# Top-k attention and a mixture of experts on one core: where the second fold and the row scatters stand in the early slots

## The chip, the core and the metric

The kernel runs on one core of a Trainium2 chip. The core has a matrix engine (PE), a vector engine (DVE), an activation engine (ACT), a general engine (POOL, also called GpSimd) and a queue for transfers (SP). Each works through its own list of instructions in a fixed order, and they meet through semaphores. What counts is the time of one execution on the device, in microseconds (us). It was 1285.07 us as the median of three runs, from 1283.54 to 1285.09.

## The reference

Two stages are computed one after the other, in float32.

- Attention over 8 batches, 8 heads, 576 positions and 64 values per head. For each row of scores the 32 largest of 576 are kept, all others are masked, and the softmax of the kept ones weighs the rows of `v`.
- A mixture of 8 experts on the 4608 resulting rows of 512 values. A gate picks one expert for each row; that expert is two matrix products (512 to 1024, relu, 1024 to 512), and the result is scaled by the gate's probability.

```python
scores = scale * np.matmul(q, k.transpose(0, 1, 3, 2))
kth = np.partition(scores, -top_k, axis=-1)[..., -top_k:-top_k + 1]
scores = np.where(scores >= kth, scores, -1000000000.0)
...
for e in range(E):
    h = np.maximum(x_sorted[lo:hi] @ w1[e], 0.0)
    y_sorted[lo:hi] = h @ w2[e]
```

## The kernel before

Two heads make a unit, so a batch has four units. The score rows of two units are cut into nine groups of two tiles of 128 rows by 576 scores; with 8 batches there are 144 groups. The loop at the end of the kernel (`loop`) takes one group per pass. A pass is called a slot here, and slots are counted from 0; slot i searches the thresholds of group i.

**The search on DVE.** The 576 scores of a row are not searched directly. `fold` (L314) takes the larger and the smaller of two halves (L320 `h`, L321 `l`, 288 wide). `fold_on` (L323) folds `h` once more: L327 puts the larger of its two halves (144 wide) into `few`, and the smaller into `hl`. The smaller half is either a minimum on DVE (L335), or, where `aside_too` is set, one sum and one difference on POOL (L332, L333), on the bits as whole numbers. `lists` (L356) then adds the eight largest of `l` and of the two halves of `hl` to `few`. `search` (L358) finds 32 maxima in four rounds: MAX8 for both tiles (L379), then MATCH_REPLACE8 for both tiles (L390), which takes the found ones out. The last MAX8 gives the threshold.

While group i is searched, the folds of group i+1 are placed in between. `behind` runs L320 and L321 ahead of the search. `then` is the second fold, `fold_on`. It stands in round 1, straight behind that round's two MAX8, if `soon` is set, and ahead of the last round otherwise.

**What follows the threshold.** ACT turns it into `low` (L401) and computes `w` (L417). POOL subtracts twice (L426, 128 by 576 each) and notes the doubtful rows (L407); at the start of the next slot it writes `nbias` (L385). ACT takes the exponent (L434), PE transposes and multiplies.

**What is fixed in order.** PE, ACT and DVE run in the order in which the loop writes their instructions. POOL's instructions are chained in that order too (`in_turn`), and its transfers are tied behind the last POOL instruction.

**The early slots.** `QUIET` is 66: in slots 1 to 65 `loose` is set. A slot is `heavy` when a unit's rows are due in it: POOL then scales the unit's logits and output rows (L519 to L524, L533) beside the search. That is so, from slot 8 on, in the slots whose number modulo 9 is 3 or 8. `k.crowded` is set by each scatter, store and block of rows. `soon` is set in an early slot that is heavy or does not follow a crowded one, and POOL takes the fold's last step where `soon` is set and the slot is not heavy, which is the case in 37 slots.

**Scatters and stores.** When a batch's four units are done, five scatters (L601, indirect transfers that POOL issues) put its rows into `x_rows`, sorted by expert. `scatter(1)` issues one at the end of each slot from slot 24, 42, 60 and so on. A finished expert block leaves its output store (L888, also POOL's) in `stores`; `put_stores` issues what is there, at the end of each slot. Pieces of the expert products fill PE beside the attention, and what is left of them runs when the attention is over.

Of the kernel before, what the change touches and what calls it, by code (L numbers as in the profile page):

```python
# [44 lines left out]
def kernel(  # L45
# [54 lines left out]
    NC = 4  # L100
# [7 lines left out]
    NT = 2 * NC + 1  # L108
# [25 lines left out]
    k = SimpleNamespace()  # L134
# [217 lines left out]
    def lists(f):  # L352

        for m in range(2):
            for j, away in enumerate((f.l[:, m, :], f.hl[:, m, 0:QF // 2], f.hl[:, m, QF // 2:QF])):
                nc.vector.max(out=f.few[:, m, QF + 8 * j:QF + 8 * j + 8], in_=away)  # L356

    def search(tiles, s, f, then=lambda: None, soon=False, behind=lambda: None, beside=lambda: None):  # L358

        m_all = range(2)  # L360
        tops = k.small.tile([P, 2, TOP_K], F32, name="tops", bufs=4)
        if k.exact:
            src = [s[:, m, :, :].rearrange("p j k -> p (j k)") for m in m_all]
            width = S
        else:
            src = [f.few[:, m, 0:QF] for m in m_all]
            width = LW
            if not f.aside:
                lists(f)
        behind()  # L370
        scr = k.att.tile([P, 2, width], F32, name="scr", bufs=1)
        nbias = k.small.tile([P, 2], F32, name="nbias", bufs=3)
        R = TOP_K // 8

        for r in range(R):
            if r == R - 1 and not soon:
                then()
            for m in m_all:
                nc.vector.max(out=tops[:, m, r * 8:(r + 1) * 8], in_=src[m])  # L379
                if r > 1:  # L380
                    tick()
            if r == 1 and soon:
                then()
            if r == 0:
                in_turn(nc.gpsimd.tensor_scalar_mul(nbias, tops[:, :, 0], -scale))  # L385
                beside()
            if r < R - 1:
                for m in m_all:
                    first = r == 0 and not k.exact
                    nc.vector.match_replace(  # L390
                        out=src[m] if first else scr[:, m, :], in_to_replace=tops[:, m, r * 8:(r + 1) * 8],
                        in_values=src[m], imm_value=NEG,
                    )
                    if r > 1:
                        tick()
                    src[m] = f.few[:, m, :] if first else scr[:, m, :]
                if first and f.aside:
                    lists(f)
        thr = tops[:, :, TOP_K - 1]
        low = k.small.tile([P, 2], F32, name="low", bufs=3)  # L400
        nc.scalar.activation(low, thr, AF.Copy, scale=STEEP)  # L401

        def doubts():
            n, i = tiles[0]
            at = n.b * U + n.u
            over = doubt[:, at:at + 2, 2 * NC, :] if tails(tiles) else doubt[:, at, 2 * i:2 * i + 2, :]
            k.last_pool = in_turn(nc.gpsimd.tensor_tensor(  # L407
                over, f.few[:, :, QF + 7:LW:8], _inner(thr, NL), op=ALU.subtract
            )).ins

        return low, nbias, doubts
# [607 lines left out]
    QUIET = 66  # L1019
# [4 lines left out]
    with fast:  # L1024
# [10 lines left out]
        waiting, loaded, coming, spare, scatters, stores = [], [], [], [], [], []  # L1035
        current = None
        left = clock = 0

        def level(b):

# [22 lines left out]
                loaded[-1].at = clock  # L1063

        def put_stores():
            while stores:
                k.crowded = True
                stores.pop(0)()

# [139 lines left out]
        def at_place(name):  # L1209
            for end in list(late):  # L1210
                if end[1] == name:
                    end[1] = next(end[0], None)
                    if end[1] is None:
                        late.remove(end)
# [18 lines left out]
        def loop():  # L1233
            nonlocal credit, rate, clock
            for i in range(min(AHEAD, len(work))):
                multiply(i)
                s_of[i], steps = scores(got_of.pop(i))
                for step in steps:
                    step()
            multiply(AHEAD)  # L1240
            for step in prepared:
                step()
            for odd in range(2):
                for h in range(2):
                    r = slice(h * D, (h + 1) * D)
                    at = odd * (lw + P) + h * E
                    nc.vector.tensor_copy(turn[r, :, at:at + E], wg[r, odd::2, :])
            f_of[0] = fold(s_of[0], (slice(0, 1), slice(1, 2)))
            fold_on(f_of[0])
            for i, (b, g) in enumerate(work):  # L1250
                tiles = tiles_of(i)
                u, tile = g[0]
                if tile == 0 and u % 2 == 0:
                    open_unit(tiles[0][0])
                if tails(tiles):
                    open_unit(tiles[1][0])

                loose = 0 < i < QUIET
                k.heavy = loose and "rows" in [place for _, place in late]
                soon = loose and (k.heavy or not k.crowded)  # L1260
                then = behind = beside = lambda: None
                if i + 1 < len(work):
                    def behind():
                        f_of[i + 1] = fold(s_of[i + 1])

                    then = lambda: fold_on(f_of[i + 1], soon and not k.heavy)
                    if i:
                        behind()
                        behind = lambda: None
                if k.heavy:  # L1270
                    beside = lambda: at_place("rows")
                held = k.heavy and k.crowded
                low, nbias, doubts = search(tiles, s_of[i], f_of.pop(i), then, soon, behind, beside)
                k.crowded, k.heavy = held, False
                at_place("small")
                w_of[i] = depths(s_of[i], low)
                less(s_of.pop(i), w_of[i])
                doubts()
                at_place("pool")
                if not loose:  # L1280
                    at_place("relu")
                    at_place("rows")
                put_stores()
                scatter(1)
                at = i % per_batch
                if at == FIRST and b:
                    rate = level(b) * PIECES / (U * NT)
                credit += rate * len(g)
                room = left
                if b == B - 1 and at >= ARRIVED:  # L1290
                    room -= KEEP
                    credit = room / (len(work) - i)
                share = {0: 0.5, 1: 1.2, 2: 1.6, 3: 0.5, 2 * NC: 1.4}[tile]
                now = max(0, min(int(credit * share + 0.5), room))
                credit -= now
                clock = i
                if i + AHEAD < len(work):
                    s_of[i + AHEAD], steps = scores(got_of.pop(i + AHEAD))
                    for step in steps:
                        step()  # L1300
                if loose:
                    at_place("relu")
                evacuate()
                at_place("turn")
                turns = turning(i - 1) if i else iter(())
                next(turns, None)
                part = min(BETWEEN, now - now // 2)
                rest = pieces(part)
                next(turns, None)
                rest = pieces(now - now // 2 - part + rest)  # L1310
                weights(tiles, w_of[i], nbias)
                next(turns, None)
                evacuate()
                if i + AHEAD + 1 < len(work):
                    multiply(i + AHEAD + 1)
                if tile == NC - 1:
                    end = ending(b, u)
                    late.append([end, next(end)])
                at_place("products")
                at_place("weights")  # L1320
                credit = min(credit + pieces(now // 2 + rest), 6 * rate)

            k.between = True
            for _ in turning(len(work) - 1):
                pieces(1)
            assert len(late) == 1
            clock = None
            for place in late[0][0]:
                if place == "rows":
                    pieces(4)  # L1330
            kept = left - (SURE + HALVES + PLAIN) * PIECES
            assert kept >= 0, kept
            k.apart = True
            pieces(kept)
# [139 lines left out]
```

## Time and profile before

| what | value |
|---|---|
| median of three runs | 1285.07 us |
| the profiled execution's own time | 1284.61 us |
| its span, first to last instruction | 1283.0 us |
| PE busy | 1176.1 us (92%) |
| DVE busy | 1058.8 us (83%) |
| ACT busy | 933.3 us (73%) |
| POOL busy | 732.0 us (57%) |
| L327, second fold, 144 times | 0.557 us on average, 0.426 to 1.535 |
| L332, POOL's first fold step, 37 times | 0.792 us on average |
| L426, POOL's subtraction, 288 times | 1.441 us on average |
| L407, doubtful rows, 144 times | 0.379 us on average |
| L601, scatter, 40 times | 1.065 us on average |
| L888, store, 37 times | 1.052 us on average |

The span is what the profile covers; the execution's own time has 1.6 us more around it. An engine is busy while one of its instructions has started and not ended, so a stalled instruction counts as busy. Instructions of one engine overlap a little at their ends. A timeline line gives the start, the time, the engine, the line of the code, what is written from what, and how many were merged; an idle time ahead of the instruction stands in brackets with what ended it.

### The profile page before, as it was taken

How to read it: one execution, taken by the hardware profiler on the slowest of the kernel's cores; microseconds unless marked ns; L12 is line 12 of the kernel's file. 1: busy time of each engine (PE TensorE's matmuls, PEld its weight loads, DVE VectorE, ACT ScalarE, POOL GpSimd, SP SyncE). 2: the span in 40 equal slices, each digit the busy share in tenths (PEclk: the TensorE clock that was granted, in tenths of full speed). 3: DMA queues.
4: the chain of work that ended last, by engine and by line, in shares of the span. 5: the costliest groups of instructions: out<-in, count | busy, mean ns of one | idle time of the engine just before them, and what ended most of it. 6: DMA issues, size and time to landing. Idle time of an engine off the chain costs nothing. (4 is left out here: it accounts for less than half of the span.)

```text
span 1283.0 us, 24461 instructions
## 1 busy us (share of the span) xinstructions
PE 1176.1 (92%) x7574; PEld 823.6 (64%) x7574; DVE 1058.8 (83%) x4608; ACT 933.3 (73%) x2136; POOL 732.0 (57%) x884
## 2 busy tenths in 40 slices
PE   6767767898899999999999999999999999999998
PEld 3444444665566566667666666666666667789975
DVE  8999999999999999999999999999999965000000
ACT  4888887988799888888788888888888872112121
POOL 4777777786678665658555855676557743101010
PEclk9888788999899999999999999999999999999999
DMA  5001113741474147533946464547555548996582
GB/s 153 31 30 31 31 39 126 263 157 39 146 251 162 39 150 283 182 135 98 332 142 218 163 224 153 189 146 264 178 178 202 172 149 285 353 358 235 215 301 83
DMA packets 98701, 220.81 MB, mean 172 GB/s; under 512 B 5309, under 2 KB 26301, under 8 KB 98560
## 3 DMA queue, kind: packets, MB, share of 16 engines
q1 hardware_dynamic: 91360, 198.87, 44.5%
q0 software_dynamic: 6384, 19.97, 4.2%
q8 instruction: 61, 1.00, 0.3%
q14 instruction: 80, 0.66, 0.2%
q10 hardware_dynamic: 816, 0.31, 0.1%
HBM read 195.75 MB, written 24.04 MB: 171 GB/s over the span
## 5 line engine op out<-in xcount | busy, mean ns | idle before, releaser
L426 POOL TENSOR_TENSOR w<-s,w 128x576 f32<-128x576 f32 x288 | 409.2, 1441 | 317.5 <-ACT w L417 317.4
L979 PE MATMUL ph<-xTs,w 128*128 128x128 f32 x2112 | 263.0, 278 | 2.6 <-ACT xTs L870 2.6
L979 PEld LDWEIGHTS ph<-xTs,w 128*128 128x128 f32 x2112 | 251.3, 194 | 21.1 <-issue 17.6
L996 PE MATMUL py<-w,hT 128*128 128x512 f32 x528 | 248.7, 600 | 1.9 <-ACT hT L984 1.6
L434 ACT ACTIVATE w<-w,nbias 128x576 f32<-128x576 f32 x288 | 223.0, 785 | 2.3 <-POOL w L426 1.4
L445 PE MATMUL wTm<-turn,w 128*128 128x128 f32 x1152 | 173.9, 291 | 52.7 <-ACT oT L484 29.1
L417 ACT ACTIVATE w<-s,low 128x576 f32<-128x576 f32 x288 | 207.7, 768 | 4.7
L304 PE MATMUL sc<-qkb 64*128 64x288 f32 (+1 forms) x1280 | 200.7, 465 | 7.8 <-DMA qkb<-in_qk_dram 4.0
L445 PEld LDWEIGHTS wTm<-turn,w 128*128 128x128 f32 x1152 | 135.1, 148 | 111.6 <-ACT oT L484 35.5
L311 ACT COPY s<-sc 128x576 f32<-128x576 f32 x288 | 168.0, 634 | 11.9 <-PE sc L304 11.8
L379 DVE MAX8 tops<-scr 128x8 f32<-128x168 f32 x576 | 169.5, 328 | 0.0
L452 ACT COPY wT<-wTm 128x512 f32<-128x512 f32 x256 | 140.7, 596 | 37.8 <-PE wTm L445 37.2
L379 DVE MAX8 tops<-few 128x8 f32<-128x144 f32 (+1 forms) x576 | 154.9, 314 | 0.0
L304 PEld LDWEIGHTS sc<-qkb 64*128 64x128 f32 (+1 forms) x1280 | 107.1, 190 | 71.5 <-issue 35.2
L996 PEld LDWEIGHTS py<-w,hT 128*128 128x128 f32 x528 | 92.0, 191 | 86.5 <-issue 83.0
L482 PE MATMUL po<-wT,vb 128*64 128x288 f32 x1024 | 143.8, 425 | 0.0
L888 POOL DMA_INDIRECT out_dram<-y,xg x37 | 38.9, 1052 | 161.3 <-ACT y L1005 82.0
L356 DVE MAX8 few<-l 128x8 f32<-128x288 f32 x288 | 129.8, 451 | 0.0
L320 DVE TENSOR_TENSOR h<-s 128x576 f32<-128x576 f32 (+1 forms) x145 | 111.7, 770 | 3.9 <-ACT s L311 3.6
L321 DVE TENSOR_TENSOR l<-s 128x576 f32<-128x576 f32 (+1 forms) x145 | 114.3, 788 | 0.0
L482 PEld LDWEIGHTS po<-wT,vb 128*64 128x64 f32 x1024 | 70.1, 141 | 68.9 <-issue 17.4
L356 DVE MAX8 few<-hl 128x8 f32<-128x72 f32 x576 | 102.3, 221 | 0.0
(205 smaller groups left out, 1596.7 us busy)
## 6 DMA issues: line engine op xcount, KB each, us to landing
w<-in_moe_w_dram SPq DMA_DIRECT2D x74, 2048.0 KB, 9.2
qkb<-in_qk_dram SPq DMA_DIRECT2D x31, 608.0 KB, 3.8
vb<-in_v_dram SPq DMA_DIRECT2D x32, 320.0 KB, 3.2
xg<-x_rows SPq DMA_DIRECT2D x37, 257.0 KB, 9.1
x_rows<-blank SPq DMA_DIRECT2D x13, 257.0 KB, 7.9
x_rows<-blank POOLq DMA_DIRECT2D x4, 257.0 KB, 9.8
x_rows<-x,posi POOLq DMA_INDIRECT x40, 3.2
out_dram<-y,xg POOLq DMA_INDIRECT x37, 3.9
```

Of the source, the lines that this page charges most:

```text
L304: nc.tensor.matmul(ps[rows, j, 0:HF], n.q[d, cols], n.k[d, keys], start=True, stop=True)
L311: lambda m=m, ps=ps: nc.scalar.copy(s[:, m, :, :], ps[:, :, 0:HF]) for m, ps in enumerate(got)
L356: nc.vector.max(out=f.few[:, m, QF + 8 * j:QF + 8 * j + 8], in_=away)
L379: nc.vector.max(out=tops[:, m, r * 8:(r + 1) * 8], in_=src[m])
L417: nc.scalar.activation(w[:, m, :], s[:, m, :, :].rearrange("p j k -> p (j k)"), AF.Relu, scale=-STEEP, bias=low[:, m:m + 1],)
L426: k.last_pool = in_turn(nc.gpsimd.tensor_tensor(w[:, m, :], s[:, m, :, :].rearrange("p j k -> p (j k)"), w[:, m, :], op=ALU.subtract)).ins
L434: nc.scalar.activation(w[:, m, :], w[:, m, :], AF.Exp, scale=scale, bias=nbias[:, m:m + 1], accum_out=n.z[:, c:c + 1])
L445: nc.tensor.transpose(pm[:, c * P:(c + 1) * P], w[:, m, first:first + P], ident)
L452: nc.scalar.copy(wT[:, :, m, q], pm4)
L482: nc.tensor.matmul(po[r, 0:HF], n.v[:, c, r], rhs, start=(c == 0), stop=(c == KC - 1))
L979: nc.tensor.matmul(ph[:, f, :], n.w1[:, 0, dt, fc * P:(fc + 1) * P], n.xT[:, dt, :], start=(dt == 0), stop=(dt == DT - 1),)
L996: nc.tensor.matmul(py, hT[:, f, :], n.w2[:, 0, f, :], start=(f == 0), stop=(f == FT - 1))
```

## The change

The code of the change has three parts, all for slots 1 to 65.

- In a slot that is not heavy and has `soon` set, the second fold stands behind round 1's two replacements, no longer ahead of them. In heavy slots it stays.
- `k.spared` is set at the end of a slot whose number modulo 9 is 2 or 7 (`NT` is 9, `NC` is 4), that is, ahead of a heavy slot. No store is issued there and no scatter; a store waits for the end of the next slot.
- With `at == 6` in the 18 slots of a batch, two scatters are issued instead of one, which makes up for the one that is left out in the slot behind it.

```diff
@@ search
-            if r == 1 and soon:
+            if r == 1 and soon and k.heavy:
                 then()
...
                 if first and f.aside:
                     lists(f)
+                if r == 1 and soon and not k.heavy:
+                    then()
@@ before the loop
         left = clock = 0
+        k.spared = False
@@ put_stores
-            while stores:
+            while stores and not k.spared:
@@ loop
+                at = i % per_batch
+                k.spared = 0 < i + 1 < QUIET and i % NT in (2, NC + 3)
                 put_stores()
-                scatter(1)
-                at = i % per_batch
+                scatter(1 if not loose else 0 if k.spared else 2 if at == 6 else 1)
```

In the two built programs PE, ACT and SP have the same instructions in the same order. On DVE 37 second folds move behind the two replacements. On POOL one scatter in each of three batches moves from ahead of a heavy slot to the end of the slot before that, where it is the second of two, and two stores move from ahead of a heavy slot to behind it.

## The prediction

> **What bounds the kernel now.** I read the page first: its 40 slices, and the busy time of the four engines in three windows (columns: window, its length, then busy us and instruction count of PE, its weight load, DVE, ACT and POOL, the granted clock, the DMA share and GB/s).
>
> ```profile
> PE   6767767898899999999999999999999999999998
> DVE  8999999999999999999999999999999965000000
> ```
>
> ```profile
> 20.00:480.00 460.00, 379.47 (x2394) 246.86 (x2396) 459.76 (x2028) 394.49 (x916) 340.99 (x410) 0.91 0.30 105
> 480.00:1047.00 567.00, 554.76 (x3736) 383.06 (x3733) 565.09 (x2414) 484.27 (x1120) 355.15 (x414) 1.00 0.54 191
> ```
>
> The first 66 slots end at 472 us. In them DVE has no gap: 459.76 of 460 us, and its waits in that window come to one, 0.2 us. So a slot there lasts as long as its DVE instructions: 6.55 us where POOL takes the fold's last step, 6.9 to 7.05 where DVE does. PE is idle for 80 us of that window and ACT for 65. But "busy" includes time in which a DVE instruction has started and cannot proceed, so I went to the timeline, engine by engine, for one ordinary slot, slot 3, counted from 0 (start and duration in us).
>
> ```profile
> 34.59 0.56 DVE L379 MAX8 tops<-few 128x8 f32<-128x168 f32 x2
> 35.06 0.45 DVE L327 TENSOR_TENSOR few<-h 128x288 f32<-128x288 f32 x1
> 35.41 0.10 DVE L390 MATCH_VALUE_LOAD scr<-tops,few 128x8 f32 x1
> 35.48 0.33 DVE L390 MATCH_REPLACE8 scr<-tops,few 128x168 f32<-128x168 f32 x1
> 35.72 0.10 DVE L390 MATCH_VALUE_LOAD scr<-tops,few 128x8 f32 x1
> 35.78 0.34 DVE L390 MATCH_REPLACE8 scr<-tops,few 128x168 f32<-128x168 f32 x1
> 36.02 0.58 DVE L379 MAX8 tops<-scr 128x8 f32<-128x168 f32 x2
> ```
>
> ```profile
> 32.24 2.83 POOL L426 TENSOR_TENSOR w<-s,w 128x576 f32<-128x576 f32 x2 [1.41 <-ACT w L417]
> 35.03 0.54 POOL L407 TENSOR_TENSOR doubt<-few,tops 128x6 f32<-128x6 f32 x1
> 35.54 0.21 POOL L385 TENSOR_SCALAR nbias<-tops 128x2 f32<-128x2 f32 x1
> 35.72 0.80 POOL L332 TENSOR_TENSOR hl<-h 128x288 int32<-128x288 int32 x1
> ```
>
> POOL's two L426 end at 35.07. L407 starts at 35.03, DVE's L327 at 35.06, and L407, which takes 0.19 where nothing disturbs it, takes 0.54: it stands still until L327 is done. The fold itself pays nothing (0.45; the least of 144 is 0.43). Two places show the opposite order. At 247.8 L327 meets a running L426 that ends at 248.42, and takes 0.91; at 359.1 DVE's L321 meets L333, POOL's second fold step, until 359.81:
>
> ```profile
> 247.83 0.91 DVE L327 TENSOR_TENSOR few<-h 128x288 f32<-128x288 f32 x1
> ```
>
> ```profile
> 358.44 1.37 POOL L333 TENSOR_TENSOR hl<-hl,few 128x288 int32<-128x288 int32 x1
> ```
>
> ```profile
> 359.07 1.36 DVE L321 TENSOR_TENSOR l<-s 128x576 f32<-128x576 f32 x1
> ```
>
> L321 normally takes 0.74, so it lost 0.62 of the 0.74 us that L333 still ran; L327 lost 0.46 of 0.60. The stall is the overlap less 0.14 us, in both. MAX8 and MATCH_REPLACE8 run beside L426 and L332 at their usual length.
>
> [...]
>
> **The change part by part.** [...]
>
> *The fold.* DVE reaches L327 by 0.29 + 0.30 + 0.24 us after the start of the second MAX8 (the steps MAX8 to replacement, replacement to replacement and replacement to the next, at 29.71, 30.00, 30.30 and 30.54): at 34.82 + 0.83 = 35.65 in this slot. What POOL does meanwhile: L407 is no longer in L327's way, takes 0.19, and nbias and L332 follow at 0.17 us each, as they do at 357.22, 357.39 and 357.56 where nothing blocks them. L332 then starts 0.31 after L426's end, at 35.38, 0.27 ahead of L327, and reads until 36.17. L327 is blocked for 0.79 - 0.27 - 0.14 = 0.38 us. Behind it on DVE stand the maxima and replacements of the last two rounds, so the threshold, and with it ACT's, POOL's and PE's work for the slot. L333, now started after L327 at about 36.5, ends at 37.35, ahead of the next L320 (38.0), and adds nothing. Nobody makes the 0.38 up.
>
> Where is POOL too late for that? From the start of L407 the trace gives it up to 48 ns of lead over L327 and lost every time; with leads of 58, 90 and 116 ns L522, L521 and L533 won. So L332, the same kind of instruction, should win with some 0.06 us of lead; nbias, a tensor_scalar, has lost with 0.14. I took the lead for each of the 37 in the same way:
> - 28 have 0.26 to 0.30: 28 x 0.38 = +10.6 us.
> - Three (slots 13, 22, 31, behind a rows slot) have 0.12: 0.53 each, +1.6.
> - Four (20, 34, 42, 60) are stalled now, by 0.27, 0.46, 0.44 and 0.37, since L426 is late from the slot before. That slot gets 0.38 longer, ACT's lateness shrinks by as much, and L332 wins by 0.08 to 0.27: 0.38 to 0.57 instead. +0.1 each, +0.4.
> - Slot 52 follows one without POOL's fold and keeps its lateness; L327 passes: -0.4, and L320 meets L333, +0.15.
> - Slot 49: L327 now falls into the second L426, +0.72, and L320 into L333, +0.4, instead of L321's 0.62: +0.5.
> - Slot 17, a rows slot, isn't edited, but its stall of 0.4 comes from slot 16's lateness (0.6), which falls by 0.38: -0.4.
>
> *The scatters.* In front of the rows of slots 26, 44 and 62:
>
> ```profile
> 192.16 1.03 POOL L601 DMA_INDIRECT x_rows<-x,posi  x1 [0.16 <-issue]
> 193.23 0.25 POOL L385 TENSOR_SCALAR nbias<-tops 128x2 f32<-128x2 f32 x1
> ```
>
> ```profile
> 194.01 0.73 DVE L320 TENSOR_TENSOR h<-s 128x576 f32<-128x576 f32 x1
> 194.66 1.81 DVE L321 TENSOR_TENSOR l<-s 128x576 f32<-128x576 f32 x1
> ```
>
> The rows (L533) start at 194.05, pushed back by the scatter, and L321 waits 1.07 for them; the same 1.81 stands in the other two batches. Without the scatter L533 runs from 192.8 to 194.05, L320 comes as it ends, and nothing stalls, as in slot 8 (L320 0.77). -3.2 us. The moved scatter issues second in the slot before, among single-input instructions; nbias gets there about 1.05 us later, still a us before L426 needs POOL. Nothing; with that cover gone 1.05 x 3. The fifth scatter, and so the tables and loads behind it, keep their slot.
>
> *The stores.* In slots 39 and 57 the store delays L533 past L320, and the rows stall DVE by about 0.07 in all. Without it L533 ends at 284.95 with L320 due at 284.60: 0.2, as in slots 12, 21 and 30 (L320 0.98 to 1.00). +0.3 for both. The store itself goes to the next slot, which has no POOL fold before or after, and lands late for nobody: the output isn't read again.
>
> The sum is 10.6 + 1.6 + 0.4 - 0.25 + 0.5 - 0.4 - 3.2 + 0.3 = +9.6 on the profiled execution's 1284.6 (span 1283.0 and 1.6 around it): 1294.2. The median shown is 0.5 above that execution: about 1294.5.
>
> Does it reach the end? From 480 on PE is busy 554.76 of 567 us and alone from 1047. A PE that carried a backlog at 480 would swallow the delay. But ACT still stands waiting for DVE's threshold in slots 61 to 64, 67 and 68 (up to 2.4 us), so PE and ACT are there no later than DVE lets them, and the order of PE is fixed. I count the delay in full.
>
> **The rivals.**
> - *DVE gets the port first.* If L332 starts 0.2 us later than I count, or L327 that much sooner, L327 wins and L332 waits. Then the 31 pay nothing (L333 ends at 37.68, L320 wants to start at 37.56, less 0.14), the four late folds save 1.54 less some 0.6, and the scatters' gain stands: -0.9 - 0.25 + 0.5 - 3.2 + 0.3 = -3.6, 1281.5 on the median. It decides between a lead of 0.06 us and none. Against it: the 0.17 us steps are measured, and the lead is four times what is needed.
> - *The port is won now by one, now by the other.* Half of the 28: 5.3 us less, about 1289. For it: the start of an instruction isn't the moment at which it asks for the port. Against: the leads are alike to 0.04 us.
> - *Absorbed.* PE's stage sets the end, and early stalls and gains vanish: about 1285. For it PE's 98%, against it ACT's waits.
>
> **How the numbers follow.** I give the forecast 0.65, DVE first 0.19, the mixture 0.08, absorption 0.08. Times within 0.2% (2.6 us) are about what a measurement of this kernel can't tell from no change. The forecast's own range is 1290 to 1299: a stall of 0.28 to 0.5 per fold. To hold 8 in 10 the range takes in the mixture, absorption and the upper part of DVE first: 1280.5 to 1299.5. Faster 0.20, same 0.10, slower 0.70.
>
> **What would show it.** Right: L327 takes about 0.83 in some 30 slots, with L332 started some 0.27 earlier than it, L407 at 0.19, ordinary slots of 6.93 us, and no L321 of 1.8 before 480. Wrong: L327 at 0.45 and L332 at more than its 0.79, or slots at 6.55. A first stage 10 us longer with an unchanged end would show absorption; later stalls of L327 of 1 us and more, from 480 on, falling otherwise would shift the end by some us unasked.

## The result, and the profile after

The changed kernel takes 1291.26 us as the median of six runs (1289.95 to 1295.78), the kernel before 1284.74 in the six runs beside them (1283.54 to 1286.28). The ratio is 1.0058, with a 95% interval of 1.0046 to 1.0071: slower by 7.5 us (5.9 to 9.1). The profiled execution took 1289.95 us, with a span of 1288.3, which is 5.3 more than before.

The page's slices of PE and DVE look as they did. A DVE that stands still counts as busy, so nothing there tells that it now stands still more often:

```profile
PE   6767666888999899999999999999999999999998
DVE  8999999999999999999999999999999975000000
```

The two windows (columns as before) show where the time goes. In the first stage DVE again has no gap, but it gets through 1993 instructions in 460 us where it got through 2028. From 480 on nothing has changed to speak of.

```profile
20.00:480.00 460.00, 374.37 (x2359) 243.23 (x2357) 460.00 (x1993) 387.66 (x901) 323.72 (x405) 0.90 0.29 100
480.00:1047.00 567.00, 555.63 (x3741) 382.16 (x3740) 565.07 (x2417) 485.87 (x1123) 352.74 (x414) 1.00 0.55 193
```

Here is DVE's timeline in slot 3, the one shown of before: the second round's MAX8 in front of the replacements, the second replacement, the fold in its new place, and the third round's MAX8.

```profile
34.39 0.55 DVE L379 MAX8 tops<-few 128x8 f32<-128x168 f32 x2
...
35.22 0.32 DVE L390 MATCH_REPLACE8 scr<-tops,few 128x168 f32<-128x168 f32 x1
35.45 0.82 DVE L327 TENSOR_TENSOR few<-h 128x288 f32<-128x288 f32 x1
36.20 0.56 DVE L379 MAX8 tops<-scr 128x8 f32<-128x168 f32 x2
```

And POOL's timeline of the same slot (L428 and L409 are the lines that were L426 and L407 before; L332 and L333 keep their numbers):

```profile
32.03 2.82 POOL L428 TENSOR_TENSOR w<-s,w 128x576 f32<-128x576 f32 x2 [1.74 <-ACT w L419]
34.82 0.20 POOL L409 TENSOR_TENSOR doubt<-few,tops 128x6 f32<-128x6 f32 x1
34.99 0.21 POOL L385 TENSOR_SCALAR nbias<-tops 128x2 f32<-128x2 f32 x1
35.16 0.79 POOL L332 TENSOR_TENSOR hl<-h 128x288 int32<-128x288 int32 x1
36.42 0.79 POOL L333 TENSOR_TENSOR hl<-hl,few 128x288 int32<-128x288 int32 x1 [0.46 <-DVE few L327]
```

L409 no longer stands still (0.54 before, 0.20 now), so L332 starts at 35.16, 0.29 ahead of L327. It runs until 35.95, 0.50 us of which fall into L327. L327 takes 0.82 where it took 0.45. The overlap less 0.14 would be 0.36; it lost 0.37. Of the 37 moved folds, 35 take more than 0.6 us; 5 did before.

Prediction and expectations call what the two contend for "the port". The traces show the times alone: one of the two stands still while the other runs (L407 before, 0.54 for 0.19, L327 now, 0.82 for 0.45). That they share a part of the chip was the author's assumption; no trace shows it. The "port theory" of the expectations says no more than that L332 goes through if it starts far enough ahead, and L327 then stands still until it is done, but for 0.14 us.

The gain that the change also brings stands in slot 26, where before L321 waited 1.07 for the rows (1.81 us). On POOL the moved scatter is now the second of two in the slot ahead. The rows (L535), with no scatter in front of them, end at 199.79, and on DVE L320 and L321 come behind them at their usual length:

```profile
190.04 1.23 POOL L603 DMA_INDIRECT x_rows<-x,posi  x1 [0.19 <-issue]
191.57 1.76 POOL L603 DMA_INDIRECT x_rows<-x,posi  x1 [0.30 <-issue]
...
198.53 1.26 POOL L535 TENSOR_TENSOR x<-xl,rz 128x640 f32<-128x640 f32 x1
```

```profile
199.94 0.74 DVE L320 TENSOR_TENSOR h<-s 128x576 f32<-128x576 f32 x1
200.60 0.75 DVE L321 TENSOR_TENSOR l<-s 128x576 f32<-128x576 f32 x1
```

To see what each slot contributes I took the end of the last MAX8 of every slot in both traces. From slot 0 to slot 65 the changed kernel loses 8.17 us:

| slots | forecast, us | measured, us |
|---|---|---|
| 28 ordinary folds | +10.6 | +10.15 |
| 13, 22, 31 (behind a rows slot) | +1.6 | +0.94 (0.33, 0.13, 0.49) |
| 20, 34, 42, 60 (L426 late before) | +0.4 | +0.99 (0.11, -0.07, 0.94, 0.01) |
| 52, with 53 | -0.25 | -0.27 |
| 49 | +0.5 | +0.54 |
| 17 | -0.4 | -0.39 |
| scatters: 26, 27, 44, 45, 62, 63 | -3.2 | -2.90 |
| stores: 39, 40, 57, 58 | +0.3 | +0.31 |
| 43 and 48, not forecast | 0 | -0.40 and -0.79 |
| all others, with rounding | 0 | -0.01 |
| sum | +9.6 | +8.17 |

Outside these slots two things differ. Slot 0 ends 0.94 us earlier in this execution. And 1.9 us are given back between slots 66 and 136, 1.1 of them in slot 70. DVE waits for nothing there, but before, its L327 met a late subtraction on POOL. These are POOL and DVE before, then DVE after:

```profile
505.13 2.79 POOL L426 TENSOR_TENSOR w<-s,w 128x576 f32<-128x576 f32 x2 [6.71 <-ACT w L417]
```

```profile
506.69 1.53 DVE L327 TENSOR_TENSOR few<-h 128x288 f32<-128x288 f32 x1
```

```profile
513.60 0.49 DVE L327 TENSOR_TENSOR few<-h 128x288 f32<-128x288 f32 x1
```

Before, L426 waited 6.71 us for ACT and ends at 507.92, 1.23 into L327; after, it waited 5.09 and ended ahead of L327. ACT in turn had waited 1.41 us for scores from PE before, and not at all after. PE was late by an expert product. First that product before, then after (PE's timelines):

```profile
491.78 4.57 PE L979 MATMUL ph<-xTs,w 128*128 128x128 f32 x24 [0.65 <-ACT xTs L870]
```

```profile
498.70 2.94 PE L981 MATMUL ph<-xTs,w 128*128 128x128 f32 x24 [0.64 <-ACT xTs L872]
```

The same 24 matmuls took 1.63 us longer before. The granted clock (the number after POOL's) was 0.72 on average in the stretch of before (0.50 from 492.25 to 495.55), and 1.00 in the stretch of after:

```profile
490.00:495.00 5.00, 3.88 (x22) 3.45 (x19) 5.00 (x23) 4.22 (x11) 2.60 (x4) 0.72 1.03 393
```

```profile
497.00:502.00 5.00, 3.88 (x32) 3.28 (x32) 5.00 (x23) 4.22 (x12) 2.51 (x4) 1.00 1.03 394
```

So the 5.3 us of the span are 8.17 - 0.94 - 1.9. The first of the three is the change, but for slot 48; the other two go with the execution at hand, as far as the runs below show.

### The profile page after: what moved, and what is told of

Same layout as the page of the kernel before. It is cut to its first block, busy times and chain, and to the rows that moved or that the text cites. A ratio compares the mean times of both kernels' runs of the same rounds, so it can differ in the third digit from the quotient of the medians.

```text
span 1288.3 us, 24461 instructions
## 1 busy us (share of the span) xinstructions
PE 1177.1 (91%) x7574; PEld 824.3 (64%) x7574; DVE 1065.3 (83%) x4608; ACT 933.5 (72%) x2136; POOL 716.5 (56%) x884
## 5 line engine op out<-in xcount | busy, mean ns | idle before, releaser
L428 POOL TENSOR_TENSOR w<-s,w 128x576 f32<-128x576 f32 x288 | 407.6, 1435 | 326.1 <-ACT w L419 324.1
L320 DVE TENSOR_TENSOR h<-s 128x576 f32<-128x576 f32 (+1 forms) x145 | 113.6, 783 | 2.7 <-ACT s L311 2.7
L321 DVE TENSOR_TENSOR l<-s 128x576 f32<-128x576 f32 (+1 forms) x145 | 108.7, 750 | 0.0
```

Of the source, the lines that this page charges most:

```text
L428: k.last_pool = in_turn(nc.gpsimd.tensor_tensor(w[:, m, :], s[:, m, :, :].rearrange("p j k -> p (j k)"), w[:, m, :], op=ALU.subtract)).ins
```

## The experiments

Two questions were open. Is it L332's lead over L327 that costs the time, or the new place of the fold by itself? And what are the scatters and the stores worth? Each ratio below is against runs of the kernel before that were made beside the run (their medians are 1283.48 to 1284.78 us); the difference in us is worked out from the ratio.

**The parts alone.** `fold_alone` is the kernel before with only the fold moved:

```diff
-            if r == 1 and soon:
+            if r == 1 and soon and k.heavy:
                 then()
...
+                if r == 1 and soon and not k.heavy:
+                    then()
```

> The kernel before with the moved fold alone; scatters and stores stay where they were. Port theory [...]: ordinary slots of 6.93 us, L327 at 0.83, the three L321 of 1.81 stay; the first stage 11 us longer than before, the time 1293 to 1295. DVE-first rival: L327 at 0.45, slots of 6.55, about 1284. Rival that the cost of the change lies in the moved scatters and stores: no difference to the kernel before, 1284.7.

Measured: 1296.32 us, ratio 1.0098 (1.0084 to 1.0113), +12.6 us. That is a little above the 1293 to 1295 expected; the forecast's terms without scatters and stores make 12.45. The three long L321 of the rows slots stay. One of them got worse. DVE and POOL in slot 26 of this run:

```profile
198.73 1.03 DVE L327 TENSOR_TENSOR few<-h 128x288 f32<-128x288 f32 x1
...
202.22 1.56 DVE L320 TENSOR_TENSOR h<-s 128x576 f32<-128x576 f32 x1
203.71 1.95 DVE L321 TENSOR_TENSOR l<-s 128x576 f32<-128x576 f32 x1
```

```profile
196.69 2.76 POOL L428 TENSOR_TENSOR w<-s,w 128x576 f32<-128x576 f32 x2 [3.43 <-ACT w L419]
199.42 0.41 POOL L409 TENSOR_TENSOR doubt<-few,tops 128x6 f32<-128x6 f32 x1
199.99 1.06 POOL L603 DMA_INDIRECT x_rows<-x,posi  x1 [0.16 <-issue]
...
201.91 1.26 POOL L535 TENSOR_TENSOR x<-xl,rz 128x640 f32<-128x640 f32 x1
```

L428 waited for ACT and ends at 199.45, 0.7 into L327. The scatter stands between it and the rows, so L535 runs from 201.91 to 203.17, into L320, and the next slot's L428 then starts into L321. The two slots to that point cost 1.6 us more than in the kernel before. With the scatter out of the way the same lateness should meet slack on POOL; `between` below shows such a place.

`spare_alone` is the opposite half: scatters and stores moved as in the changed kernel, the fold left in place.

```diff
-            while stores:
+            while stores and not k.spared:
...
-                put_stores()
-                scatter(1)
                 at = i % per_batch
+                k.spared = 0 < i + 1 < QUIET and i % NT in (2, NC + 3)
+                put_stores()
+                scatter(1 if not loose else 0 if k.spared else 2 if at == 6 else 1)
```

> The kernel before with the scatter and store part alone. Port theory: L321 behind the rows of slots 26, 44 and 62 falls from 1.81 to 0.74, 3 x 1.07 us, and L320 in slots 39 and 57 loses 0.15 each: 2.9 us less, 1281.8. Rival (the scatters hold nothing up that counts): 1284.7. Rival (two scatters in a row hold the slot behind them up by about 1 us): 3 us less and 3 us more, 1284.7.

Measured: 1282.88 us, ratio 0.9993 (0.9983 to 1.0004). The three L321 stalls are gone (1.05 us each), and in the trace the stage is 2.1 us shorter, but the time isn't shown to differ from that of before. So the halves don't add up: +12.6 and -0.9, against +7.5 together. I split this half once more. `scatters_alone` moves the three scatters and leaves the stores:

```diff
-                put_stores()
-                scatter(1)
                 at = i % per_batch
+                put_stores()
+                k.spared = 0 < i + 1 < QUIET and i % NT == NC + 3
+                scatter(1 if not loose else 0 if k.spared else 2 if at == 6 else 1)
```

> The kernel before with the three scatters moved and the two stores left in front of the rows. Port theory: 3 x 1.07 = 3.2 us less than before, 1281.5, and 0.3 us less than with the stores moved too, which the time can't tell apart; in the trace L320 of slot 39 stays near 0.77. Rival (the stores are what counts): 1284.7.

Measured: 1281.56 us, ratio 0.998 (0.997 to 0.9989): -2.6 us, near the forecast's term of -3.2. `stores_alone` moves the two stores only:

```diff
-            while stores:
+            while stores and not k.spared:
...
+                at = i % per_batch
+                k.spared = 0 < i + 1 < QUIET and i % NT in (2, NC + 3)
                 put_stores()
```

> The kernel before with only the two stores moved from ahead of a heavy slot to behind it; folds and scatters stay. The prediction's term for the stores (+0.3 us, DVE meeting the end of L533 in slots 40 and 58) gives 1.0002, about 1285. If instead the stores cost what separates the run with scatters and stores moved from the run with the scatters alone moved (0.9993 against 0.998), this one gives 1.0013, +1.7 us.

Measured: 1286.46 us, ratio 1.0014 (1.0006 to 1.0022): +1.8 us, as the difference of the two runs above foretold. In its trace the two edited places cost 0.14 and 0.15, as forecast. Other delays come up in slots that aren't edited (6, 8 and 11, by 0.41, 0.73 and 0.42): L327 took 0.85, 1.16 and 0.86 there, since POOL's subtractions ended 0.5 to 0.9 later than in the kernel before. On the other side the three long L321 are gone, though the scatters stand where they were. DVE, then POOL, at the rows of slot 26:

```profile
196.86 0.73 DVE L320 TENSOR_TENSOR h<-s 128x576 f32<-128x576 f32 x1
197.51 0.74 DVE L321 TENSOR_TENSOR l<-s 128x576 f32<-128x576 f32 x1
```

```profile
196.89 2.49 POOL L533 TENSOR_TENSOR x<-xl,rz 128x640 f32<-128x640 f32 x1
```

L533 starts just behind L320, as it did before (194.05 behind 194.01). Before, it went on when L320 had ended (1.80 us; undisturbed it takes 1.26), and L321 waited (1.81); here it stands still for both. The traces with unmoved scatters have thirteen such places: in nine L533 starts 38 to 58 ns behind L320, and L321 takes 1.8; in four it starts 30 to 39 ns behind, and L321 takes 0.74 (the three here and one in `pad`). The two groups lie a hundredth of a microsecond apart: the scatter brings L533 to an edge at which it may or may not cost a microsecond. In this trace the gains and the delays nearly cancel by slot 65; why the median loses 1.8 and not 0.3 is not settled.

**The lead turned round.** If L332's lead is the cause, the fold can stay in its new place and cost nothing, as long as L332 comes later. `pool_later` is the changed kernel with `nbias` written three times, which holds L332 back by two more of these small instructions:

```diff
-                in_turn(nc.gpsimd.tensor_scalar_mul(nbias, tops[:, :, 0], -scale))
+                for _ in range(3 if soon and not k.heavy else 1):
+                    in_turn(nc.gpsimd.tensor_scalar_mul(nbias, tops[:, :, 0], -scale))
```

> The changed kernel with POOL made slower: where POOL takes the fold it writes nbias three times instead of once, the same values, which puts L332 about 0.34 us later. Port theory: L332 then comes to the port just behind L327, L327 falls to about 0.45 and ordinary slots to 6.55 to 6.6 us; with the gain of the scatters about 1281 to 1282.5, nearly 10 us less than the changed kernel although POOL has more to do. Rival (behind the replacements the fold itself costs DVE more, by a dependence or a lost overlap): 1291. Rival (POOL's time counts): above 1291.

Measured: 1283.93 us, ratio 1.0005 (0.9996 to 1.0013), somewhat above the 1281 to 1282.5 expected. Slot 3 on DVE and on POOL:

```profile
36.16 0.44 DVE L327 TENSOR_TENSOR few<-h 128x288 f32<-128x288 f32 x1
```

```profile
35.68 0.99 POOL L386 TENSOR_SCALAR nbias<-tops 128x2 f32<-128x2 f32 x3
36.64 0.78 POOL L332 TENSOR_TENSOR hl<-h 128x288 int32<-128x288 int32 x1
```

More work on POOL, and the kernel is 6.8 us faster than the changed one. L327 goes through at 0.44 while POOL's third `nbias` stands still for it (the three take 0.99; one takes 0.21, and at steps of 0.17 three would take 0.55), and L332 starts after it. The ordinary slots last 6.65: 0.1 more than before, since L333 ends at 38.30 and the next L320, at 38.08, takes 0.83 and not 0.73.

**Past the lead.** If it is the overlap that costs, a place so late that L332 is done is free too. `two_max` puts the fold behind the third round's two MAX8. From the changed kernel:

```diff
             for m in m_all:
                 nc.vector.max(out=tops[:, m, r * 8:(r + 1) * 8], in_=src[m])
+                if r == 2 and soon and not k.heavy and m == 1:
+                    then()
...
-                if r == 1 and soon and not k.heavy:
-                    then()
```

> The changed kernel with the second fold moved on by two more MAX8, behind the third round's maxima. Port theory: L327 comes 0.48 us later, at the end of L332 (started 0.27 + 0.48 = 0.75 us earlier, 0.79 long), and is not stalled: L327 about 0.45, slots of 6.55, 1281 to 1282.5. Rival (the later the fold, the dearer): 1291 or more.

Measured: 1281.02 us, ratio 0.9975 (0.9967 to 0.9983); L327 0.43, ordinary slots 6.55. L332 is done at 35.58 in slot 3, as L327 starts:

```profile
35.56 0.43 DVE L327 TENSOR_TENSOR few<-h 128x288 f32<-128x288 f32 x1
```

```profile
34.78 0.80 POOL L332 TENSOR_TENSOR hl<-h 128x288 int32<-128x288 int32 x1
36.13 0.79 POOL L333 TENSOR_TENSOR hl<-hl,few 128x288 int32<-128x288 int32 x1 [0.56 <-DVE few L327]
```

This is the changed kernel with the fold two MAX8 further on and nothing else changed. Its ratio is 0.0083 lower, which is 10.7 us: about what the folds' stalls were summed to.

`one_max` puts it behind the first of these MAX8 (`m == 0` in the line above).

> The changed kernel with the second fold moved on by one MAX8. Port theory: L332 leads by 0.27 + 0.24 = 0.51 us, so L327 is stalled by 0.79 - 0.51 - 0.14 = 0.14 us in some 31 slots: slots of 6.69, L327 about 0.59, 4 us above the unstalled version, 1285 to 1287. Rival (a fixed cost of any place behind the replacements): 1291.

Measured: 1284.19 us, ratio 0.9994 (0.9986 to 1.0002), just under the range expected. L332 is 0.55 ahead of L327 in slot 3 and reads 0.26 us into it:

```profile
36.71 0.58 DVE L327 TENSOR_TENSOR few<-h 128x288 f32<-128x288 f32 x1
```

```profile
36.16 0.81 POOL L332 TENSOR_TENSOR hl<-h 128x288 int32<-128x288 int32 x1
```

L327 loses 0.14, and slots are 0.15 longer than before. The overlap less 0.14 is 0.12. One rule, fitted on two places of the kernel before, thus gives the stall at overlaps of 0.50 and 0.26 us.

`between` goes the other way: it puts the fold ahead of the second replacement of round 1, where it starts together with L332.

```diff
                 for m in m_all:
...
                         in_values=src[m], imm_value=NEG,
                     )
+                    if r == 1 and soon and not k.heavy and m == 0:
+                        then()
...
-                if r == 1 and soon and not k.heavy:
-                    then()
```

> The changed kernel with the second fold between round 1's two replacements. Port theory: L327 comes 0.30 us sooner than in the changed kernel, 0.03 ahead of L332, and wins: about 0.45, slots of 6.55, 1281 to 1282.5. If the lead counts otherwise than from the starts, L332 wins and L327 is stalled by about 0.6: 1297.

Measured: 1280.52 us, ratio 0.9969 (0.9958 to 0.9979). In slot 3 both start at the same hundredth, and this time DVE goes through:

```profile
34.82 0.45 DVE L327 TENSOR_TENSOR few<-h 128x288 f32<-128x288 f32 x1
```

```profile
34.82 1.10 POOL L332 TENSOR_TENSOR hl<-h 128x288 int32<-128x288 int32 x1
36.00 0.80 POOL L333 TENSOR_TENSOR hl<-hl,few 128x288 int32<-128x288 int32 x1
```

L332 takes 1.10 where it took 0.79, that is 0.31 more, which is L327's 0.45 less 0.14: the same rule with the sides exchanged. POOL has time for it; L333 ends at 36.80, ahead of L320 at 37.04. What was the rival "DVE gets the port first" is 0.3 us of lead away from the change (0.29 there, none here), and its price was right: 1281.5 was worked out for it, and the run gives 1280.5.

**Does a delay there reach the end?** `pad` is the kernel before with the last MAX8 of each of the 37 searches done twice; it works out the same values again.

```diff
+        if soon and not k.heavy:
+            nc.vector.max(out=tops[:, 1, TOP_K - 8:TOP_K], in_=src[1])
```

> The kernel before with one MAX8 done twice, the same values, at the end of each of the 37 slots in which POOL takes the fold: a delay of DVE of 0.24 us each, 8.9 us in all, without any port. If early DVE time passes to the end in full, the time rises by 8.9 less about 1.2 that the late slots give back (L426 less late by 0.24 in slots 17, 20, 34, 42 and 60): about 1292.4. If PE's stage absorbs a part, by less: 1285 to 1289.

Measured: 1297.56 us, ratio 1.0104 (1.0089 to 1.012), +13.4 us. The extra MAX8 is L400 here, in slot 3:

```profile
38.00 0.56 DVE L379 MAX8 tops<-scr 128x8 f32<-128x168 f32 x2
38.59 0.34 DVE L400 MAX8 tops<-scr 128x8 f32<-128x168 f32 x1
38.84 0.74 DVE L320 TENSOR_TENSOR h<-s 128x576 f32<-128x576 f32 x1
```

It doesn't follow at the usual step of 0.24: it starts 0.03 after its predecessors have ended, and the slot is 0.37 longer, by chance the same as with the fold's stall. 37 times 0.13 more than expected is most of the 5 us by which the run lies above the 1292.4 written down. The early stage is 10.7 us longer in the trace, and the span 11.2. So a delay of about this size on DVE in these slots passes through to the end whole; PE's busy second stage absorbs none of it.

**Whether the better place and the scatters add up.** `between_alone` has the fold between the replacements and leaves scatters and stores as before; `between_scatters` has that fold and the moved scatters, without the moved stores. The first against the kernel before:

```diff
-            if r == 1 and soon:
+            if r == 1 and soon and k.heavy:
                 then()
...
+                    if r == 1 and soon and not k.heavy and m == 0:
+                        then()
```

> The kernel before with only the 37 folds moved, to between round 1's two replacements; scatters and stores stay in front of the heavy slots. L332 and L327 start within 0.05 us of each other there, and in the earlier run with the folds in this place DVE's fold went through at 0.45 us. That run was at 0.9969 with the scatters and stores moved; the scatters' own run is at 0.998. If the parts add up, this one gives 0.999, -1.3 us, and its ordinary slots last 6.55 us as before; the gain would be in the few slots in which L426 is late. If the place of the fold carries the whole gain, it gives 0.997.

The second against `between`:

```diff
-            while stores and not k.spared:
+            while stores:
...
-                k.spared = 0 < i + 1 < QUIET and i % NT in (2, NC + 3)
                 put_stores()
+                k.spared = 0 < i + 1 < QUIET and i % NT == NC + 3
```

> The folds between round 1's two replacements and the three scatters moved; the two stores stay ahead of their heavy slots. If the stores' move costs 0.3 us, this gives 0.9967, about 1280.3; if it costs 1.7, 0.9956, about 1279. Above 0.998 the scatters and this place of the fold do not add up.

Measured: `between_alone` 1285.72 us, ratio 1.0003 (0.9995 to 1.0012); `between_scatters` 1279.85 us, ratio 0.9969 (0.9957 to 0.9981). The place alone gains nothing; with the scatters out of the way it does, and with or without the stores it is 0.3% faster than before. The trace of `between_alone` shows in slot 26 what `fold_alone` showed there: L327 1.03, L320 1.57, L321 1.95. `between` has the same late L428 in slot 26 (the slot is 0.67 longer), but without a scatter between it and the rows the next slot costs nothing more. Three traces agree on this; that it makes up the whole difference of 4.4 us between `between` and `between_alone` isn't shown. That the stores cost 1.8 alone and nothing measurable in this company isn't explained either.

**The give-back at slot 70.** In thirteen traces, the two kernels' and the eleven above, six have no stretch of half clock on PE between 489 and 506 us (the changed kernel, `fold_alone`, `pool_later`, `two_max`, `one_max`, `between`). Against the kernel before they all win 1.1 us in slot 70, and 0.9 to 1.9 from slot 66 to 136. The other six, and the kernel before, have one of 3.4 us, beginning between 489 and 503; they win at most 0.11 in slot 70. It goes with the clock: `between` and `between_scatters`, which differ by two stores long before, stand on different sides. That the edit has no part in it isn't shown, since all five traces with the fold behind both replacements are among the six.

## Why the prediction was right

The forecast was about 1294.5 and slower (its terms make 1294.6); the measured 1291.26 lies in the forecast's own range (1290 to 1299). By its steps:

- *L332 goes first, by 0.26 to 0.30, and L327 is blocked for 0.38.* Right: the lead's median is 0.27, L327's 0.84, and L409 takes 0.19 to 0.21 in the ordinary slots; ordinary slots last 6.93. 28 x 0.38 was 10.6 and measured 10.15; 26 of the 28 have 0.36 to 0.46. The other two are slots 18 (+0.54) and 50 (-0.29).
- *The stall is the overlap less 0.14.* Right in kind, and 0.12 is nearer: the second of the two places that it was fitted on gives 0.12 already (0.74 less 0.62). In the two kernels' traces up to 480 us there are 72 places where L327, L320 or L321 waits for a POOL tensor_tensor that started ahead of it, with overlaps of 0.17 to 1.19 us. Against undisturbed lengths of 0.44, 0.73 and 0.74 the loss is the overlap less 0.11 to 0.13 in each.
- *The threshold of about 0.06 us of lead.* Right for the places at hand, but not a rule: in `fold_alone` L332 won with 0.048, and in `one_max` a subtraction (L428) with 0.115 and L526, a step of the logits, with 0.112 lost. In the changed kernel it was tested by chance. Of the three slots behind a rows slot, to which I gave a lead of 0.12 and +0.53 each, slot 31 had just that, and L332 won. Slot 22 had 0.04, and DVE won. DVE, then POOL, in slot 22:

```profile
168.14 0.46 DVE L327 TENSOR_TENSOR few<-h 128x288 f32<-128x288 f32 x1
```

```profile
168.10 1.15 POOL L332 TENSOR_TENSOR hl<-h 128x288 int32<-128x288 int32 x1
```

  The same two in slot 31:

```profile
233.53 0.98 DVE L327 TENSOR_TENSOR few<-h 128x288 f32<-128x288 f32 x1
```

```profile
233.41 0.79 POOL L332 TENSOR_TENSOR hl<-h 128x288 int32<-128x288 int32 x1
```

  So the term of 1.6 was mis-sized; it measured 0.94. I had taken one lead for all three.
- *The four late slots, +0.1 each.* Mis-sized. Three of them came to 0.05 together, and slot 42 cost 0.94, since L327, 1.44 us long there, met a late L428.
- *Slots 17, 49 and 52, scatters and stores.* Right to 0.3 us each: -0.39, +0.54, -0.27, -2.90 and +0.31. `scatters_alone` bears the scatters out by time (-2.6), but the term was in part luck: `stores_alone` has the scatters unmoved and no such stall, so the 1.81 is not what this place always costs. The stores' time alone (+1.8) is larger than the term, and the reason is open.
- *Slot 48 was no term, and gave -0.79.* It is a stall of the kernel before's own execution: L327 took 1.20 there. Ten of the eleven experiments don't have it either, whatever they change (their slot 48 is about 0.77 shorter than that of before). A single trace of before was taken to be what before always does.
- *The delay counts in full to the end.* Right as a mechanism: `pad` shows it, and nothing of the 8.17 us is absorbed by PE. The span's 5.3 is smaller by the start and the clock; the runs' ratio puts the whole at 7.5. The forecast had named stalls of L327 from 480 on that fall otherwise as what could shift the end, and slot 70 was one.

That the changed kernel came out 2 us better than the forecast by the ratio (7.5 against 9.6) is the stage's 1.4, and a remainder within the interval. On the parts the forecast was too simple in one way: it added scatters and fold. Measured, the scatters and stores are worth 0.9 us beside the unmoved fold, and about 5 beside the moved one (12.6 less 7.5). The part of that which a trace explains is the rows slot with a scatter ahead of it, which has no slack left for a late L428.

The forecast took it from three places in the trace of before (0.54, 0.91 and 1.36 us) that the one that goes first runs through and the other stands still for it; that this holds at the new place too was an assumption. In slot 3 the runs show it from both sides: L327 blocked in the changed kernel (0.82 for 0.45), L332 blocked in `between` (1.10 for 0.79). One thing the assumption doesn't foretell: where L533 waits behind L320 it shows a start 0.62 us ahead of L321, and in four of thirteen places L321 still goes first.

Of the versions run, `between` (0.9969) and `between_scatters` (0.9969) beat both kernels, and so do `two_max` (0.9975) and `scatters_alone` (0.998): the change's idea of clearing the rows' way is worth keeping, with the fold one replacement earlier or two maxima later.

## What to carry to other kernels

Where instructions of two engines stand still for each other, as L327 and those of POOL did here, moving one can free the other engine and so let it go first: work out for the new place who starts first, and by how much, before looking at what the old place cost. Here 0.3 us of lead, or a place behind the other's instruction, was worth more than the idea behind the move. And what slack on a helper engine is worth depends on what lateness meets it: the same three scatters gave 2.6 us beside the unmoved fold and 4.4 beside the fold between the replacements.

## What the runs showed of the hardware that was not expected

- In the kernel before, a stretch of 3.4 us at half the granted TensorE clock (0.50 from 492.25 to 495.55) came with a loss of DVE time though DVE waited for nothing. The 24 matmuls took 4.57 us there and 2.94 at full clock; ACT and POOL's subtraction came 1.6 us late, and the subtraction met L327 (1.53 for 0.49). In the traces without such a stretch the end of slot 136 came 0.9 to 1.9 us sooner than in the kernel before.
- In the traces of the two kernels the stretches at half clock last 3.41 us or a whole multiple of it (the last of each trace 4.37 and 4.40), and they begin whole multiples of 3.413 us apart. Counted in pieces of that length, between 30 and 1000 us, 31 pieces at full clock were followed by one at half clock; PE was busy for 0 to 1.84 us of each. 486 were followed by one at full clock, with 1.58 us or more. Ahead of the product above, the piece from 488.79 had 1.84 us in the kernel before, and that from 494.09 had 2.31 in the changed one. What sets the clock these counts don't show.
- The MAX8 that writes the output of the MAX8 ahead of it once more, in slot 3 of `pad`, cost 0.37 us where the usual step is 0.24: it started 0.03 after its predecessor's end.
- A few hundredths of a microsecond of lead decided which one stood still: with 0.04 us (slot 22 of the changed kernel, L332 1.15), or none (slot 3 of `between`, 1.10), POOL's L332 lost to DVE; with 0.12 (slot 31, L327 0.98) it won. The exceptions above (0.048 won, 0.115 lost) show that the starts in a trace don't tell the order to the hundredth.
- POOL's L533, waiting for one DVE instruction, was passed over by the next one too: it took 2.49 us behind L320 and L321 in `stores_alone`, and 1.80 behind L320 alone in the kernel before.
